# Key-block stores of an attention and key-mix kernel: ACT's DMA queue against SP's

## The chip, the cores and the metric

The kernel runs on one core of a Trainium2 chip. The metric is the device time of one execution in microseconds (us); lower is better. Engines carry the names of the profile: PE (TensorE, matmuls), PEld (its weight loads), DVE (VectorE), ACT (ScalarE), POOL (GpSimd) and SP (SyncE, which here issues DMAs only). SPq and ACTq stand for what an engine's own queue does, such as issuing a DMA.

## What is computed

All data is float32. Attention with a tanh cap runs over 8 batches, 12 heads, 448 positions and 64 columns; its output, with the heads side by side, is the input `x` (448 x 768 per batch) of a gated channel mix.

```python
scores = cap * np.tanh(np.matmul(q, k.transpose(0, 1, 3, 2)) / np.sqrt(64) / cap)
attn = np.exp(scores - np.max(scores, axis=-1, keepdims=True))
x = np.matmul(attn / (np.sum(attn, axis=-1, keepdims=True) + 1e-09), v)
# heads side by side: x is 8 x 448 x 768; x_prev is x one position earlier
xk = mu_k * x + (1.0 - mu_k) * x_prev
xr = mu_r * x + (1.0 - mu_r) * x_prev
k = np.maximum(xk @ w_k, 0.0)
v = k * k @ w_v
out = 1.0 / (1.0 + np.exp(-(xr @ w_r))) * v
```

## The kernel before

**Steps.** The attention part works on 48 pairs of heads (8 batches, six pairs each). `step(i)` (line 818) walks a string of operation names and calls the method of each name, most for pair i and some for an earlier pair: the values' matmuls (V), `gather`, `recip` and `rec_store` for pair i-1, `norm` and the mixes for i-2, `x_store` and `gate_new` for i-3 (lines 824 to 827). Within an engine's queue the order is that of the strings. From step 14 to step 47 the string is made by `rows(i % 6)` out of ROWS and ROWS_PE (lines 64 to 68 and 90 to 92): a prefix such as `25:` keeps a name only where i % 6 is one of these digits, and the PE work of a step stands in two places of the string. Steps 15, 21, 27, 33, 39 and 45 have i % 6 = 3; steps 18, 24, 30, 36 and 42 have 0; steps 14, 20, ... have 2 and 17, 23, ..., 47 have 5.

**A pair's own work.** PE computes transposed scores of four key groups (`scores`, line 261; the first three are L275, the rest of two pairs together L268) into two score buffers, ACT applies tanh (L288) and exp (L301), and PE multiplies with the values (`values`, L312 and L328) into one of two output buffers. DVE's transposing reduction (`red`, L337) sums the exponentials. Four small DMAs on SP gather the sums (`gather`, L343), DVE adds and inverts them (`recip`, lines 347 to 354), SP stores the reciprocals (`rec_store`, L357) and loads them back, spread over all partitions (`rec_load`, L366, two DMAs, at the end of the step). `norm` (L370) of the next step multiplies the output by them. `mix_old` (ACT, L380) and `mix_new` (DVE, L385) form `xk` and free the output buffer of pair i-2, which the values of pair i need. POOL and DVE form the gate's row `xg` (L403, L397), and `x_store` (L414) stores it from SP.

**Key blocks.** The first matrix product of the mix (`xk @ w_k`) runs inside the same steps, one batch late. `krow` (line 473, matmuls L486) multiplies three terms per product in halves of 64 rows and builds key blocks in pairs, in two buffers (`kps`). When a pair of blocks is done, `relu` (ACT, L497) takes it to one of four SBUF tiles `ko` of 128 x 448, and `k_store` (ACT's queue, L503) stores each tile to `k_d` in DRAM, 224 KB. After step 47 the rest of the key matmuls follows, and then the second part (the tail): Strassen-like products of the squared keys and of the gates' rows (L693), with the output stores.

**Weights.** The weights come as 64-bit floats, and steps 0 to 11 and 14 to 41 each turn one piece into float32: `weight_load` (SP, L528), `weight_abs` (ACT, L535), five DVE operations drawn one at a time by the `f` of the string (L559 to L568), a sum on POOL (L575) and `weight_store` (SP, L598) at the end of the step.

**What sets the order around the change.** In steps 15, 18, 21, ... , 45 (i % 6 of 0 and 3) ACT's queue has `relu`, `k_store`, `weight_abs` and then tanh of the next step. In steps 14, 17, ..., 47 (2 and 5) it has `relu` and `k_store` ahead of `mix_old` or tanh 2. SP's queue has, in each step: `load_v`, four `gather`, `weight_load`, `x_store`, `rec_store`, `load_qk`, two `rec_load`, `weight_store`. The steps are counted by their `rec_store`: that of step 24 is issued at 269.87 us of the span, that of step 27 at 304.75 us.

Of the kernel before, what the change touches and what calls it, by code (L numbers as in the profile page):

```python
# [17 lines left out]
B, H, S, D = 8, 12, 448, 64  # L18
# [43 lines left out]
weight_abs load_qk rec_load quad_load tail_open weight_store"""  # L62
EVEN = ODD.replace("V S2", "V S3 S2").replace(" red3", "").replace("tanh2", "tanh3 tanh2").replace("K relu k_store prep\n", "K exp3 red3 relu k_store prep\n")
ROWS = """load_v gather quad_load weight_load PE 135:red3 f f f f f gate_new tanh0 exp0 red0
weight_sum tanh1 exp1 25:relu 25:k_store red1 norm recip x_store rec_store qk_high qk_low 2:mix_old 024:tanh3 tanh2 01345:mix_old mix_new x_high x_low gate_old
exp2 red2 weight_rest weight_sum 024:exp3 024:red3 03:relu 03:k_store weight_abs load_qk rec_load quad_load weight_store PE_END"""
ROWS_PE = (("S1 V S3 S2 K18", "N0 N1 K15"), ("drain V S2 K15", ""), ("S0 S1 W K6 T S3 S2 K18", ""),
           ("S0 S1 V S2 K18", "N0 N1 K12"), ("drain V S3 S2 K18", ""), ("S0 S1 drain V K6 S2 N0 K18", ""))
STEP_0 = """gather rec_load load_v x_store weight_load S0 S1 V0 S2 V1 S3 V2 V3 f f f f f tanh0 exp0 red0
# [39 lines left out]
class Body:  # L109
# [394 lines left out]
        self.ko = []  # L504

    def key_piece(self, n):
        if n < 2 * NARROW:
            return n // 2, range(n % 2 * ND // 2, (n % 2 + 1) * ND // 2)  # L510
        if n >= NWK - 2:
            return (NF - 1, range((n - NWK + 2) * ND // 2, (n - NWK + 3) * ND // 2)) if n < NWK else None
        return n - NARROW, range(ND)
# [544 lines left out]
```

## Time and profile before

| | before |
|---|---|
| median of 3 runs (lowest, highest) | 940.9 us (938.95 to 942.15) |
| the profiled execution, its own time | 941.72 us |
| span of its profile | 939.8 us |
| PE, DVE, ACT, POOL busy, share of the span | 94%, 77%, 66%, 44% |
| ACT's stores of key blocks (L503) | 64 |
| mean granted clock of PE, as a share of full speed | 0.99 |

The span is the time from the first to the last instruction of the profiled execution; the 1.9 us between it and that execution's time lie around it. An engine's share of busy time is a mean over the attention steps (to about 545 us), the rest of the key blocks (to about 580 us) and the tail, which differ. In what follows, "who waited for whom" rows give the total, the number of times and the longest wait; a wait is put down to the event that ended it.

### The profile page before, as it was taken

The page shows a single profiled execution, that of the slowest core. Times are in us where ns is not written, and L with a number is a line of the kernel's source. Part 1 is how long each engine was busy: PE and PEld are TensorE (multiplying, and loading weights), DVE is VectorE, ACT ScalarE, POOL GpSimd, SP SyncE. Part 2 cuts the span into 40 slices and gives each one's busy share as a digit, 9 for nine tenths or more (in the row PEclk, how much of TensorE's full clock was granted, in tenths as well). Part 3 has the DMA queues.
Part 4 walks back from the last instruction along what each step waited for, and adds up shares of the span by engine and source line. Part 5 has one row for each costly group of instructions (what it writes and reads, how often), then busy time and mean ns, then how long its engine had stood idle before and what let it go on. Part 6 is the DMA issues. An engine that isn't in the chain of part 4 may idle for free.

```text
span 939.8 us, 16780 instructions
## 1 busy us (share of the span) xinstructions
PE 883.4 (94%) x5826; PEld 708.8 (75%) x5826; DVE 720.8 (77%) x1246; ACT 622.9 (66%) x907; POOL 409.0 (44%) x345
## 2 busy tenths in 40 slices
PE   7889999899899999999999899999999999999997
PEld 3236667566666666666666589999999999999996
DVE  6888976779779778777868674688878766777775
ACT  8988877667767767776866665655656544555553
POOL 5986565657657667667655200000000013334430
PEclk9999999999999999999999899999999999999999
DMA  5465655575566666657556463754544636767663
GB/s 171 154 214 170 215 157 165 177 211 166 186 205 175 181 192 181 195 174 213 165 156 189 139 227 108 258 158 154 178 146 150 195 120 190 231 204 216 219 214 121
DMA packets 123678, 170.14 MB, mean 181 GB/s; under 512 B 22592, under 2 KB 107712, under 8 KB 123584
## 3 DMA queue, kind: packets, MB, share of 16 engines
q1 hardware_dynamic: 114224, 154.10, 54.0%
q10 hardware_dynamic: 9360, 14.88, 4.3%
q8 instruction: 48, 0.79, 0.4%
q14 instruction: 46, 0.38, 0.1%
HBM read 109.91 MB, written 56.60 MB: 177 GB/s over the span
## 4 chain that ended last, share of the span: by engine, by line
PE 45%; DVE 21%; DMA 17%; ACT 6%; SPq 5%; issue 4%; ACTq 1%; POOL 0%; DVEq 0%
PE ps L693 38%; DVE r L337 7%; DMA r<-rec_d 6%; DMA sq__194<-r 5%; DMA rec_d<-rs 4%; PE kps L462 4%; SPq L343 3%; ACT p L288 3%; ACT p L301 2%; DVE x L370 2%; SPq L366 2%; DVE sq__194 L347 1%; DVE wsq L559 1%; DVE wa L564 1%; DVE wa L562 1%
## 5 line engine op out<-in xcount | busy, mean ns | idle before, releaser
L337 DVE TRANSPOSE_TENSOR_REDUCE r<-p 128x28 f32<-128x896 f32 (+1 forms) x192 | 181.4, 972 | 19.2 <-ACT p L301 18.5
L288 ACT ACTIVATE p<-s,scl_t 128x896 f32<-128x896 f32 (+1 forms) x172 | 166.0, 977 | 27.0 <-PE s L275 7.4
L301 ACT ACTIVATE p<-p,cap_t 128x896 f32<-128x896 f32 (+1 forms) x172 | 174.3, 1023 | 4.3 <-ACT ko L497 0.4
L312 PE MATMUL pv<-p,rv 128*64 128x448 f32 x576 | 126.2, 566 | 21.9 <-DVE xk L385 18.2
L693 PE MATMUL ps<-wvh,hi 128*128 128x384 f32 x392 | 131.0, 334 | 0.0
L693 PE MATMUL ps<-wvl,hi 128*128 128x384 f32 x392 | 130.9, 334 | 0.0
L657 POOL TENSOR_TENSOR s<-src 128x384 f32<-128x384 f32 x14 | 14.2, 1018 | 267.6 <-DVE lo L678 267.6
L486 PE MATMUL kps<-xkh,wkh 64*128 64x448 f32 (+1 forms) x540 | 119.0, 373 | 7.9 <-ACT ko L497 7.9
L677 ACT CAST hi<-s 128x512 fp32r<-128x512 f32 (+1 forms) x112 | 63.6, 568 | 88.7 <-PE ps L693 78.0
L486 PE MATMUL kps<-xkh,wkl 64*128 64x448 f32 (+1 forms) x540 | 116.3, 367 | 0.0
L486 PE MATMUL kps<-xkl,wkh 64*128 64x448 f32 (+1 forms) x540 | 115.1, 364 | 0.0
L678 DVE TENSOR_TENSOR lo<-s,hi 128x512 fp32r<-128x512 f32 (+1 forms) x112 | 70.1, 626 | 57.4 <-ACT hi L677 43.4
L133 POOL TENSOR_TENSOR qkl<-rqk,qkh 128x896 fp32r<-128x896 f32 x47 | 100.2, 2133 | 10.7 <-ACT qkh L127 7.2
L312 PEld LDWEIGHTS pv<-p,rv 128*64 128x64 f32 x576 | 39.4, 140 | 83.4 <-issue 51.3
L575 POOL TENSOR_TENSOR wsq<-wa,wsq 128x384 f32<-128x384 f32 (+1 forms) x40 | 54.2, 1356 | 104.9 <-DVE wsq L568 93.9
L693 PE MATMUL ps<-wrh,hi 128*128 128x384 f32 x294 | 98.6, 335 | 0.3 <-DVE o L716 0.3
L693 PE MATMUL ps<-wrl,hi 128*128 128x384 f32 x294 | 98.5, 335 | 0.0
L677 ACT CAST hi<-src 128x512 fp32r<-128x512 f32 (+1 forms) x84 | 47.7, 567 | 62.1 <-PE ps L693 59.2
L486 PEld LDWEIGHTS kps<-xkh,wkh 64*128 64x128 f32 (+1 forms) x540 | 65.2, 186 | 24.7 <-ACT ko L497 12.7
L693 PE MATMUL ps<-wvh,lo 128*128 128x384 f32 x392 | 83.7, 334 | 0.0
L275 PE MATMUL s<-qkh 64*128 64x448 f32 x288 | 62.0, 418 | 16.0 <-ACT p L288 11.4
L693 PEld LDWEIGHTS ps<-wvh,hi 128*128 128x128 f32 x392 | 73.6, 188 | 0.1
(117 smaller groups left out, 1917.5 us busy)
## 6 DMA issues: line engine op xcount, KB each, us to landing
rqk<-qk SPq DMA_DIRECT2D x47, 448.0 KB
k_d<-ko ACTq DMA_DIRECT2D x64, 224.0 KB
src<-k_d SPq DMA_DIRECT2D x56, 256.0 KB
rv<-v SPq DMA_DIRECT2D x48, 256.0 KB
r<-rec_d SPq DMA_DIRECT2D x96, 112.0 KB
v_d<-o SPq DMA_DIRECT2D x56, 192.0 KB
src<-x_d SPq DMA_DIRECT2D x42, 256.0 KB
vl<-v_d SPq DMA_DIRECT2D x56, 192.0 KB
```

The source lines that it names most:

```text
L133: {"p": self.nc.gpsimd, "v": self.nc.vector}[e].tensor_sub(*a)
L275: nc.tensor.matmul(s[:, (h + i) % 2, 0:S], qk[a][p, k], qk[b][p, 0:S], start=(n == 0), stop=(n == 2))
L288: self.nc.scalar.activation(p32[:, n], self.S.pop((i, g))[:, n, 0:S], AF.Tanh, scale=self.scl_t)
L301: self.nc.scalar.activation(p32, p32, AF.Exp, scale=1.0 if self.maxima else self.cap_t)
L312: nc.tensor.matmul(pv[p, 0:S], v[:, g, h, :], ph[:, (h + i) % 2, :], start=(g == 0), stop=False)
L337: self.nc.vector.tensor_reduce(out=r1[:, 0:RM].rearrange("p (x g) -> p x g", g=3)[:, :, g] if g < 3 else r1[:, RM:RC], in_=p32.rearrange(" ...
L462: nc.tensor.matmul(self.kps[fc][:, 0:S], w, m[:, dc, :], start=first, stop=last)
L486: self.nc.tensor.matmul(self.kps[c][:, 0:S], w[p, dc, c * P:(c + 1) * P], m[p, dc, :], start=s == 0, stop=last or way == 2 and t == 2, ski ...
L575: {"p": self.nc.gpsimd, "v": self.nc.vector}[e].tensor_add(sq, f(a), sq)
L677: self.nc.scalar.copy(hi, x)
L678: self.nc.vector.tensor_sub(lo, x, f(hi))
L693: self.nc.tensor.matmul(o, a[:, c, :], w[:, c, :], start=first and k == 0, stop=last and k == len(todo) - 1, skip_group_check=True)
```

## The change

In steps 14 to 47 the key blocks' stores go out on SP's DMA queue. In steps 14, 17, ..., 47 they follow the `rec_store` of the same step. The blocks that `relu` takes in steps 15, 18, ..., 45 are kept until the next step and are stored there between `x_store` and `rec_store`. `relu` keeps its places. Steps before 14 and after 47 store from ACT's queue as before.

```diff
 ROWS = """load_v gather quad_load weight_load PE 135:red3 f f f f f gate_new tanh0 exp0 red0
-weight_sum tanh1 exp1 25:relu 25:k_store red1 norm recip x_store rec_store qk_high qk_low 2:mix_old 024:tanh3 tanh2 01345:mix_old mix_new x_high x_low gate_old
-exp2 red2 weight_rest weight_sum 024:exp3 024:red3 03:relu 03:k_store weight_abs load_qk rec_load quad_load weight_store PE_END"""
+weight_sum tanh1 exp1 25:relu red1 norm recip x_store 14:k_put rec_store 25:k_put qk_high qk_low 2:mix_old 024:tanh3 tanh2 01345:mix_old mix_new x_high x_low gate_old
+exp2 red2 weight_rest weight_sum 024:exp3 024:red3 03:relu weight_abs load_qk rec_load quad_load weight_store PE_END"""
...
+    def k_put(self):
+        for b, fc, ko in self.ko:
+            self.nc.sync.dma_start(self.k_d[fc, :, b * S:(b + 1) * S], ko)
+        self.ko = []
```

## Rows read from the trace of the kernel before

**Rows 1.** The page, part 1: busy time and share of the whole span.

```profile
PE 883.4 (94%) x5826; PEld 708.8 (75%) x5826; DVE 720.8 (77%) x1246; ACT 622.9 (66%) x907; POOL 409.0 (44%) x345
```

**Rows 2.** Busy time by window: steps 20 to 42, then the tail.

```profile
core 0: us, PE busy (x) PEld busy (x) DVE busy (x) ACT busy (x) POOL busy (x), PEclk, DMA share, GB/s
...
236.00:487.00 251.00, 231.85 (x1870) 163.17 (x1872) 195.63 (x342) 182.16 (x225) 166.06 (x131) 0.99 0.62 186
...
580.00:940.00 360.00, 352.90 (x2035) 352.20 (x2033) 269.88 (x487) 193.07 (x374) 59.96 (x56) 1.00 0.58 182
```

**Rows 3.** The chain of waits, 262 to 330 us: start, us, what.

```profile
269.87 1.89 DMA rec_d<-rs
...
272.31 3.19 DMA r<-rec_d
...
275.58 0.34 ACTq L503
...
276.51 0.50 ACT wsq L535
...
277.09 1.02 ACT p L288
...
304.75 1.55 DMA rec_d<-rs
...
306.86 4.03 DMA r<-rec_d
...
310.96 0.33 ACTq L503
```

**Rows 4.** Timeline of ACT about step 24's end: start, us, line, [idle before].

```profile
269.35 0.95 ACT L497 ACTIVATE ko<-kps 128x448 f32<-128x448 f32 x2
275.58 0.83 ACTq L503 DMA_DIRECT2D k_d<-ko  x2
276.51 0.54 ACT L535 ACTIVATE wsq<-w 128x384 f32<-128x384 f32 x1 [6.21 <-DMA w_d<-wsq]
```

**Rows 5.** Groups by line and shape, 166 to 510 us, with idle before.

```profile
L559 DVE TENSOR_SCALAR wsq<-wsq 128x384 f32<-128x384 f32 x27 | 15.5, 575 | 45.5 <-ACT wsq L535 45.5
...
L535 ACT ACTIVATE wsq<-w 128x384 f32<-128x384 f32 x27 | 14.7, 545 | 49.0 <-DMA r<-rec_d 26.7 <-DMA w_d<-wsq 22.4
```

**Rows 6.** What PE waited for, 150 to 580 us: total, times, longest.

```profile
PE s L275 <- ACT p L288: 9.7, 10, 1.8
PE pv L312 <- DVE xk L385: 9.7, 5, 3.8
PE kps L486 <- ACT ko L497: 7.9, 6, 1.9
PE s L268 <- ACT p L288: 2.3, 4, 0.8
```

**Rows 7.** Busy time by window: granted clock about step 24, and before it.

```profile
264.00:298.00 34.00, 31.98 (x252) 22.66 (x244) 25.61 (x45) 23.22 (x29) 22.50 (x18) 0.95 0.65 185
298.00:332.00 34.00, 30.69 (x252) 22.25 (x250) 27.38 (x51) 25.73 (x33) 22.54 (x18) 1.00 0.64 187
```

**Rows 8.** Timeline of SP, steps 25 and 26.

```profile
280.04 0.33 SPq L414 DMA_DIRECT2D x_d<-xg  x1
284.19 0.36 SPq L357 DMA_DIRECT2D rec_d<-rs  x1
...
293.86 0.33 SPq L357 DMA_DIRECT2D rec_d<-rs  x1
294.32 0.33 SPq L204 DMA_DIRECT2D rqk<-qk  x1
296.26 1.12 SPq L366 DMA_DIRECT2D r<-rec_d  x2
```

**Rows 9.** DMA queues, 166 to 510 us: packets, MB, share of 16 engines.

```profile
q1 hardware_dynamic: 33592, 53.93, 54.2%
q10 hardware_dynamic: 5760, 9.18, 7.3%
```

## The prediction

> **What bounds the kernel now.** I read the busy totals first: TensorE is busy 94% of the span, VectorE 77%, ScalarE 66% [rows 1]. The table by window says where the missing 6% lies: in the tail (580 to 940 us) PE is busy 352.9 of 360 us, but in steps 21 to 42 only 231.85 of 251 us [rows 2]. So the attention steps, where the moved stores are, hold some 19 us of idle PE per 251 us, and no other engine is full there (DVE 195.6, ACT 182.2 of 251).
>
> The chain of waits says what the idle is made of [rows 3]. Around step 24 it hardly touches PE. It runs from the store of the reciprocals (269.87) to their broadcast load, 3.19 us in flight, and from its landing to the **issue of a key block's store on ACT's queue** at 275.58; then weight_abs and the first tanh of the next step run on ACT, DVE follows, and at 304.75 the next such reciprocal store begins the same round. Three steps pass in one round: 34.9 us.
>
> That edge looks odd, since a store of relu's output has nothing to do with the reciprocals. ACT's timeline shows it bare: both relus end at 270.3, the two stores are issued from 275.58 on, and weight_abs has waited 6.21 us [rows 4]. In the program every DMA counts on one of eight completion semaphores and first waits for the last DMA that used the same one; they are dealt out by a timing estimate, by which the stores of steps 15, 18, ... come after that step's rec_load and weight_store. So ACT, whose next work (weight_abs, tanh 0, exp 0) needs none of it, stands still until a DMA has landed that SP issued later. From 166 to 510 us this costs ACT 49.0 us before nine weight_abs, 5.4 us each, and DVE's weight splitting waits 45.5 us behind it [rows 5]. Steps 42 and 45 have the same wait ahead of tanh; eleven in all.
>
> What PE loses is less, since it has matmuls to run meanwhile [rows 6]: 9.7 us in ten waits plus 2.3 in four for a tanh to free a score buffer, and 9.7 in five for mix_new (xk) to free an output buffer. I placed these waits: the fourteen for tanh all come in the step after a stall; four of the five for xk (all but the longest, 3.8 us, at 536 us) come one step later, where DVE is still late. The 7.9 us for relu fall ahead of the stalls of steps 15, 21, ... and are PE's own turn from one pair of key blocks to the next.
>
> **The change, part by part.** *Removed from ACT:* 47 issues (11 stalled pairs; 11 pairs and one triple in steps 14, 17, ... 47). A pair takes 0.83 us of its queue [rows 4]; the stall is the larger part. Terms on PE's path:
> - waits for tanh: 9.7 + 2.3 = 12.0 us go;
> - waits for xk: 9.7 - 3.8 = 5.9 us go, since DVE's weight work starts some 5 us earlier;
> - the clock: after the 1.8 us wait at step 25 the matmuls ran slow; the window 264 to 298 us was granted 0.95, the next one 1.00 [rows 7]. 0.05 x 34 = 1.7 us go.
>
> Together 19.6 us. The unstalled pairs of steps 14, 17, ... sit beside other waits (behind them ACT waits for DVE or for PE's scores, and no PE wait of the list follows them): nothing.
>
> Can the other engines follow? A round without the 5.4 us would need 34.9 - 5.4 = 29.5 us; PE needs 231.85/251 x 34.9 = 32.2 us. So **PE becomes the bound**, with 2.7 us of slack in the round of the reciprocals. ACT's idle falls, but it stays under 80%.
>
> *Added to SP:* 47 issues. A 224 KB row store, the nearest row, takes 0.33 us to issue [rows 8]. In steps 16, 19, ... the pair goes between x_store and rec_store, where SP idles from 280.4 to 284.2 waiting for the reciprocals: 3.8 us hide some 0.8. Queued behind the pair are rec_store and all later SP work; the relu it needs ran a step earlier. In steps 14, 17, ... the pair follows rec_store, and load_qk, rec_load, weight_store, load_v and the next gather stand behind it; SP has 1.6 us before rec_load, which waits for rec_store's landing anyway (load_qk ends at 294.65, rec_load starts at 296.26). Relu ran about 4 us before rec_store there (step 26: it ends by 289.7). So the issues cost 0, and 0.4 us a store if the cover goes.
>
> The completion semaphores turn harmless: with all DMAs of these steps on one queue, the user before is the eighth DMA earlier on SP itself, most of a step back.
>
> *Moved transfers.* ACT's queue moved 40 stores with 7.3% of 344 us of all 16 engines [rows 9], 0.63 us each, 1.26 a pair. On SP's queue they stand in line ahead of the small transfers of the round. From below it costs nothing (the pair has gone while SP idles); from above one pair per three steps lies wholly on the path, 11 x 1.26 = 14 us. A gain is excluded, since the bytes are the same. I take 4 us, nearer to nothing, because the two gaps on SP and the 2.7 us of slack are each larger than 1.26.
>
> The sum: 941.7 (span 939.8 and 1.9 around it) - 19.6 + 4 = 926.1 us. The profiled execution is 0.8 above the median of 940.9, so I forecast **925 us**. Its own range: 941.7 - 19.6 - 0.8 = 921 with no cost, 917 if earlier relus also halve the 7.9 us of PE's turns; 935 with the 14 us.
>
> A rule speaks against this. The Trainium skill, "DMA: Bandwidth & Descriptors", "Issuing engines are not separate DMA queues", holds that starting DMAs on several engines saves only the sequencer's issue time, usually small; the change would then take 47 x 0.4 = 19 us off an ACT that has 27% to spare, and the sum would stay at 941. The trace differs: the queue lost 5.4 us a pair, not 0.8, to a wait. What the rule would give is rival 2.
>
> **Rivals.**
> 1. *The reciprocals' transfers take over part of it.* If queueing takes more than the 2.7 us of slack, waits for tanh go but V waits for xk after every second round: 941 - 12.0 - 1.7 + 4 + about 2 = 933, up to 938. For it: the chain is made of these transfers. Against it: the gaps on SP. 12%.
> 2. *Nothing changes.* ACT's freed time is slack, or the wait travels with the store and SP stands where ACT stood, rec_store behind it: 941. Against it: the chain runs through the stalled issue, and x_store is issued at 280.04, so a wait there would have to be for something issued a step before. 8%.
> 3. *Slower.* Key bytes delay rec_store in one step and rec_load with the next gather in another. With the queues at 54.2 + 7.3 = 62% busy [rows 9], a pair leaves in 1.26/0.38 = 3.3 us; twice per round is 6.6, more than the 5.4 freed. The point is 5.4 us lost per round; at 6.6 it is 11 x 1.2 = 13 us slower, 954. Against it: the pairs start while SP waits on DVE, so part of the 3.3 has passed. 6%. The same page, "Queues, rings and completion order", says that each DMA engine takes a queue's descriptors in ring order and alternates between queues by packet, so small transfers would lose the way past that they have now. No row of before shows it, as these stores never shared SP's queue.
>
> **How the numbers follow.** My forecast has 74%, the rivals 12, 8 and 6. The likeliest is 925 with 917 to 935 of its own; stretched to most of rival 1 the range is 917 to 938 and leaves out some 2 in 10. A measurement of this kernel can tell about 0.3% (2.8 us) from no change. Faster by more: 74 + 12 = 86%; within it 8%; slower 6%.
>
> **What the profile after would show.** Right: no ACT idle of 5 us ahead of weight_abs; DVE's wait for it gone with it; the L275 and L268 waits for tanh mostly gone; PE busy near 97% in the steps; a round near 32.5 us; the tail unchanged. SP's waits ahead of rec_store shorter by the two issues. Wrong: SP waiting 4 us at the new store; r<-rec_d or the gather landing later and x (L370) waiting for it; new PE waits for xk in the steps after 14, 17, .... If ACT's stalls go and PE's idle stays, my step from ACT to PE is what failed.

## The result: 911.05 us, 3.1% faster

| | before | after |
|---|---|---|
| median of 4 runs (lowest, highest) | 939.92 us (938.67 to 942.15) | 911.05 us (909.07 to 913.83) |
| the profiled execution, its own time (span) | 941.72 us (939.8) | 913.83 us (912.0) |
| time after / before, 95% interval | | 0.9692 [0.9658, 0.9727] |

The sign and the mechanism were right; the size was not. I forecast 925 with a range of 917 to 938, and the kernel came out 6 us below the range: a gain of 29 us where I had summed up 16.

The page of the changed kernel, parts 1 and 4 (busy totals, and the chain that ended last by engine):

```profile
PE 880.1 (97%) x5826; PEld 710.1 (78%) x5826; DVE 728.1 (80%) x1246; ACT 623.8 (68%) x907; POOL 409.2 (45%) x345
...
PE 68%; DVE 12%; DMA 9%; ACT 5%; SPq 2%; issue 2%; POOL 0%; DVEq 0%; ACTq 0%; POOLq 0%
```

Against [rows 1], PE rose from 94% to 97% of a shorter span, and PE is now 68% of the chain (45% before). Ten rounds of three steps lie between the rec_store of step 15 and that of step 45; the table by window over just these, for the kernel before and then for the changed one:

```profile
166.69:510.25 343.56, 316.01 (x2550) 221.43 (x2550) 267.99 (x466) 250.81 (x309) 224.50 (x178) 1.00 0.62 185
```

```profile
165.41:484.38 318.97, 313.94 (x2555) 223.46 (x2557) 276.68 (x466) 251.81 (x309) 224.56 (x177) 0.99 0.66 198
```

The columns are those of [rows 2]: window, length, then busy PE, PEld, DVE, ACT, POOL, the clock, DMA share and GB/s. Ten rounds went from 343.6 to 319.0 us, **34.4 to 31.9 us a round**. PE's idle in them fell from 343.56 - 316.01 = 27.6 to 5.0 us, and its busy time by 2.1 us. What is left of the 27.8 us between the spans: 1.3 us was there before step 15 was reached (that point varies between 164.2 and 167.7 us over the runs below, so it is chance), and 1.9 us come later. That last stretch, from the rec_store of step 45 to the end, varies between 425.2 and 430.0 us over the runs, and the run below in which every stall stands has 427.7 there, against 429.6 before and 427.6 after: the 1.9 us are not told from chance either.

ACT's timeline at the end of step 24, as in [rows 4]:

```profile
261.38 0.95 ACT L497 ACTIVATE ko<-kps 128x448 f32<-128x448 f32 x2
262.22 0.56 ACT L540 ACTIVATE wsq<-w 128x384 f32<-128x384 f32 x1
262.67 1.01 ACT L288 ACTIVATE p<-s,scl_t 128x896 f32<-128x896 f32 x1
```

Relu, weight_abs (now L540) and tanh follow each other without a gap, where 6.21 us stood. The groups by line from 165 to 484 us say the same of all steps, as [rows 5] did for before:

```profile
L564 DVE TENSOR_SCALAR wsq<-wsq 128x384 f32<-128x384 f32 x27 | 19.9, 736 | 0.1
L540 ACT ACTIVATE wsq<-w 128x384 f32<-128x384 f32 x27 | 14.8, 548 | 0.0
```

Of the 49.0 us of ACT and the 45.5 us of DVE nothing is left. What PE waits for from 160 to 515 us, as in [rows 6]:

```profile
PE kps L486 <- ACT ko L497: 3.2, 3, 1.6
PE pv L312 <- DVE xk L385: 3.1, 2, 2.8
```

The waits for tanh (9.7 + 2.3 us) are gone altogether, those for xk are down to one long one in the last steps, and those for relu fell from 7.9 to 3.2, which I had not expected. SP in steps 25 and 26, as in [rows 8], the new stores being L510:

```profile
270.87 0.83 SPq L510 DMA_DIRECT2D k_d<-ko  x2
273.16 0.37 SPq L357 DMA_DIRECT2D rec_d<-rs  x1
273.62 0.35 SPq L204 DMA_DIRECT2D rqk<-qk  x1
...
283.03 0.34 SPq L357 DMA_DIRECT2D rec_d<-rs  x1
283.46 0.80 SPq L510 DMA_DIRECT2D k_d<-ko  x2
284.35 0.41 SPq L204 DMA_DIRECT2D rqk<-qk  x1
284.86 1.12 SPq L366 DMA_DIRECT2D r<-rec_d  x2
```

A pair takes 0.8 us of SP. In step 25 SP still waits from 271.7 to 273.2 for the reciprocals; in step 26 rec_load now starts right behind load_qk. The old gap there is used up, but not overdrawn.

### The profile page after: what moved, and what is told of

It reads as the page before. It is cut to its first block, busy times and chain, and to the rows that moved or that the text cites. A ratio compares the mean times of both kernels' runs of the same rounds, so it can differ in the third digit from the quotient of the medians.

```text
span 912.0 us, 16778 instructions
## 1 busy us (share of the span) xinstructions
PE 880.1 (97%) x5826; PEld 710.1 (78%) x5826; DVE 728.1 (80%) x1246; ACT 623.8 (68%) x907; POOL 409.2 (45%) x345
## 4 chain that ended last, share of the span: by engine, by line
PE 68%; DVE 12%; DMA 9%; ACT 5%; SPq 2%; issue 2%; POOL 0%; DVEq 0%; ACTq 0%; POOLq 0%
PE ps L698 39%; PE kps L486 10%; PE pv L312 7%; DVE r L337 5%; PE s L275 4%; PE kps L462 4%; DMA r<-rec_d 3%; DMA sq__194<-r 3%; ACT p L288 2%; SPq L343 2%; ACT p L301 2%; DMA rqk<-qk 2%; PE pv L328 1%; DMA rec_d<-rs 1%; PE s L268 1%
## 5 line engine op out<-in xcount | busy, mean ns | idle before, releaser
L683 DVE TENSOR_TENSOR lo<-src,hi 128x512 fp32r<-128x512 f32 (+1 forms) x84 | 56.7, 675 | 21.4 <-ACT hi L682 19.3
```

Source lines behind the costliest of these rows:

```text
L683: self.nc.vector.tensor_sub(lo, x, f(hi))
```

## Experiments

My theory: the whole gain is that ACT no longer waits for a DMA that is issued later, and the queue on which the stores go is of no matter. The rivals: the gain is ACT's issue time; or the stores had to leave ACT's queue; and, for the size, that the moved bytes cost something. Each run is named by what it does; the first four ran beside the kernel before at 938.27 us.

**Only the stalled pairs, or only the others.** The operations of ROWS that differ from the changed kernel, first run and second:

```diff
-25:relu red1 norm recip x_store 14:k_put rec_store 25:k_put qk_high
+25:relu 25:k_store red1 norm recip x_store 14:k_put rec_store qk_high
```

> Only the pairs of steps 15, 18, ..., 45 go out on SP (one step later); those of steps 14, 17, ..., 47 are issued on ACT as before. Wait theory (all the gain is ACT no longer standing 5 us until rec_load or weight_store has landed): 23 of 47 stores moved bring nearly all of it, 909 to 915 us, and ACT's wait ahead of weight_abs is gone. Issue theory (the gain is ACT's time for issuing 47 stores): about half, 922 to 929.

Measured 912.27 us, ratio 0.9731 [0.9705, 0.9758].

```diff
-x_store 14:k_put rec_store 25:k_put qk_high
+x_store rec_store 25:k_put qk_high
...
-03:relu weight_abs
+03:relu 03:k_store weight_abs
```

> Only the stores of steps 14, 17, ..., 47 go out on SP, behind rec_store; the pairs of steps 15, 18, ... stay on ACT. Wait theory: the stalls stay, ACT idles some 5 us ahead of nine weight_abs, 935 to 942 us. Issue theory: about half of the gain, 922 to 929.

Measured 937.69 us, ratio 1.0001 [0.9981, 1.002]. ACT's waits from 160 to 515 us in it (total, times, longest):

```profile
ACT wsq L540 <- DMA r<-rec_d: 26.5, 5, 5.7
ACT wsq L540 <- DMA w_d<-wsq: 20.9, 4, 5.9
ACT p L288 <- DMA rv<-v: 6.3, 1, 6.3
ACT p L288 <- DMA r<-rec_d: 4.6, 1, 4.6
```

All eleven stalls stand there, 58.3 us, and 25 stores taken off ACT's queue bought nothing. The 22 stores of the other kind (the 23 of the expectation is a miscount; the last triple is left on ACT) bring it all: within the intervals the first run is as fast as the changed kernel. The issue theory falls.

**The same without SP.** From the kernel before:

```diff
-weight_sum tanh1 exp1 25:relu 25:k_store
+weight_sum tanh1 exp1 14:k_store 25:relu 25:k_store
...
-03:relu 03:k_store weight_abs
+03:relu weight_abs
```

> All stores stay on ACT's queue; the pairs of steps 15, 18, ... are issued one step later, behind exp 1, where the DMAs whose completion they wait for were issued most of a step before. Wait theory: it is the wait and not the queue, so most of the gain comes without SP, 911 to 920 us, the rest being 0.8 us of issue a pair. Theory that the stores must leave ACT's queue (issue time, or two queues in each other's way): no gain, 935 to 942.

Measured 910.45 us, ratio 0.9706 [0.9679, 0.9732]. ACT's timeline at the same place:

```profile
261.07 0.98 ACT L497 ACTIVATE ko<-kps 128x448 f32<-128x448 f32 x2
261.94 0.56 ACT L535 ACTIVATE wsq<-w 128x384 f32<-128x384 f32 x1
...
266.11 1.93 ACTq L503 DMA_DIRECT2D k_d<-ko  x2
268.92 1.01 ACT L288 ACTIVATE p<-s,scl_t 128x896 f32<-128x896 f32 x1 [2.48 <-PE s L275]
```

The pair is issued on ACT's own queue at 266.1, where ACT would wait for PE's scores anyway. So no store had to change its queue: what counts is that it is issued where the DMA it has to wait for is already done. SP is one such place.

**The wait put back without a store.** The changed kernel, with a small copy on ACT that waits for rec_load (the old stalls ended with the landing of rec_load or of weight_store, which is issued behind it):

```diff
+    def peek(self):
+        t = self.up.tile([P, 8], F32, name="peek", bufs=1)
+        self.nc.scalar.copy(t, max(self.R.items())[1][:, 0:8])
...
-03:relu weight_abs load_qk rec_load quad_load
+03:relu 1245:weight_abs load_qk rec_load 03:peek 03:weight_abs quad_load
```

> The changed kernel with all stores on SP, and in steps 15, 18, ..., 45 ACT copies eight columns of the freshly loaded reciprocals just ahead of weight_abs, so that it waits for rec_load as before but issues no store. Wait theory: the loss comes back, ACT idle near 5 us a step with it, PE waits for tanh near 12 us, for xk near 6 and for relu near 7, 934 to 942 us. If the gain came from the stores' queue or their issue: 911 to 916.

Measured 926.21 us, ratio 0.9874 [0.985, 0.9899]: between the two, so neither expectation held. The waits of ACT and then those of PE, 160 to 515 us:

```profile
ACT peek L510 <- DMA r<-rec_d: 48.0, 11, 5.4
```

```profile
PE kps L486 <- ACT ko L497: 6.5, 5, 1.3
PE pv L312 <- DVE xk L385: 6.3, 5, 1.4
PE s L275 <- ACT p L288: 4.9, 7, 1.2
```

The wait that I put back is smaller than the old one: 48.0 us in eleven, with the copy 4.6 us each, where the old stalls took 58.5 us, 5.3 each, store issue included. The loss came back in the same three places, the waits for relu among them (6.5 us, where the changed kernel has 3.2); those go with the stall. But 86% of the stall brought back only 15 of 29 us. That pointed to two limits: a round lasts the longer of what PE needs and of what the round of the reciprocals needs with the stall in it, and the first part of a stall is free.

**A stall of a chosen length.** The changed kernel with four, then eight dummy copies on ACT in the place of the old wait:

```diff
+    def filler(self):
+        if not self.scr:
+            self.scr.append(self.up.tile([P, S], F32, name="scr", bufs=1))
+            self.nc.gpsimd.memset(self.scr[0], 0.0)
+        for _ in range(4):
+            self.nc.scalar.copy(self.scr[0], self.scr[0])
...
-03:relu weight_abs
+03:relu 03:filler weight_abs
```

> The changed kernel with four dummy copies on ACT (128 x 448, some 0.55 us each, 2.2 us together) ahead of weight_abs in steps 15, 18, ..., 45, in the place of the old wait. Two-limits theory: a round lasts the longer of PE's 31.9 us (measured after the change) and 29.0 us (the 34.4 of before less its 5.3 of stall) plus what ACT loses there; 2.2 us stay under the slack of 2.9, so 910 to 916. Theory that every us lost there costs its 11 us: 934.

> The same with eight copies, some 4.4 us: 29.0 + 4.4 = 33.4, 1.5 over PE's 31.9, eleven times: 16 us, 924 to 932. Theory that every us costs: 958. Theory that PE hides it: 911 to 915.

Measured 914.48 us (0.9745 [0.9715, 0.9776]) and 933.23 us (0.9944 [0.9924, 0.9965]), beside 938.34 of before. One copy took 0.57 us. The first 2.3 us a round cost some 3.5 us in all (its interval just overlaps that of the changed kernel), the next 2.3 us cost 18.8. Eight were 1 us above my band. The mean of ten rounds (rec_store of step 15 to that of step 45), against "29.0 plus the loss, or PE's 31.9, whichever is longer", where 29.0 is 34.4 less 5.3:

| kernel | ACT loses a round | the rule gives | measured |
|---|---|---|---|
| before | 5.3 us | (set) | 34.4 us |
| the wait put back | 4.6 | 33.6 | 33.3 |
| eight copies | 4.5 | 33.5 | 34.0 |
| four copies | 2.3 | 31.9 | 32.1 |
| changed | 0 | (set) | 31.9 |
| stores later on ACT | 0 | 31.9 | 31.5 |

The rule holds within 0.5 us. Part of that is scatter: a second profile of the changed kernel, of the last set of runs below, gave 31.6 us a round.

**The price of the moved bytes.** Every moved block stored twice, the second time to a scratch tensor:

```diff
             self.nc.sync.dma_start(self.k_d[fc, :, b * S:(b + 1) * S], ko)
+            self.nc.sync.dma_start(self.k_e[fc, :, b * S:(b + 1) * S], ko)
```

> The changed kernel, each key block of steps 14 to 47 stored twice on SP (the second time to a scratch tensor): twice the issues and bytes ahead of rec_store, rec_load and the gather. Theory that the moved transfers cost nothing, because the round of the reciprocals has slack: 910 to 915 us. Theory that the 4 us of the forecast are real and hidden behind other gains: one more pair costs at least 4, up to 14 us, 915 to 926.

Measured 928.65 us, ratio 0.9901 [0.9871, 0.9932], 17.6 us more than the changed kernel (which was measured in another set of runs; by the two ratios it is 19.6) and above both bands. DVE's waits in it and then PE's, 160 to 515 us:

```profile
DVE sq__195 L347 <- DMA sq__195<-r: 27.2, 19, 2.4
DVE x L370 <- DMA r<-rec_d: 5.5, 8, 1.6
```

```profile
PE kps L486 <- ACT ko L497: 12.2, 7, 3.2
PE pv L312 <- DVE xk L385: 1.6, 4, 0.6
```

In the changed kernel the first of these was 19.8 us (5.9 before the change) and the second absent:

```profile
DVE sq__194 L347 <- DMA sq__194<-r: 19.8, 20, 2.0
```

So the small transfers of the round do come later with twice the stores, DVE's norm (L370) waits for them, and PE waits 12.2 us for relu. SP in step 26 of this run, to be read against the changed kernel's rows above:

```profile
290.78 0.34 SPq L357 DMA_DIRECT2D rec_d<-rs  x1
...
293.09 1.49 SPq L204 DMA_DIRECT2D rqk<-qk  x1
294.67 1.12 SPq L366 DMA_DIRECT2D r<-rec_d  x2
```

From rec_store to rec_load SP needs 3.89 us here, and 1.83 in the changed kernel: the four stores take their issue time, and load_qk's issue behind them takes 1.49 us in place of 0.41. So the run doubles issues and bytes at once, and does not tell which of the two makes the round late.

What one pair's bytes do can be read from the traces by timing rec_load from its issue to its landing (the last count on its completion semaphore), in the mean of steps 17, 20, ..., 44. It took 3.30 us before the change, 4.57 in the changed kernel, where a pair stands in line ahead of it, and 4.29 with the doubled stores; where no pair stands between rec_store and rec_load (the places exchanged, stores later on ACT), 3.4 to 3.6. So a pair in line delays rec_load by some 1.3 us, close to the 1.26 of the prediction's upper bound, and at the single dose the round's slack hides it.

**The place on SP**, with the two places exchanged:

```diff
-x_store 14:k_put rec_store 25:k_put
+x_store 25:k_put rec_store 14:k_put
```

> The changed kernel with the order on SP turned round: the stores of steps 14, 17, ... ahead of rec_store, those of 16, 19, ... behind it. Theory that the place on SP does not matter within the slack: 909 to 914 us. Theory that it was chosen on an edge: 915 or more, with SP waiting ahead of rec_store or rec_load longer.

Measured 908.74 us, ratio 0.9676 [0.9646, 0.9706]. It looked 2 us better, so it ran again beside three others, all on one chip, with the kernel before at 940.33 us. The fourth has the stores ahead of step 14 and behind step 47 on SP too (`k_store` with `nc.sync` for `nc.scalar`).

> The changed kernel once more, on the chip of the next three: 907 to 914 us. It is the yardstick for them.

> The turned order on SP (stores of steps 14, 17, ... ahead of rec_store, of 16, 19, ... behind it) once more. Theory that the place on SP does not matter: within 0.3% of the changed kernel. Theory that the place takes the last of PE's idle: 2 to 3 us faster, as it looked.

> All stores on ACT's queue, the stalled pairs a step later, once more. Theory that the queue does not matter, only the wait: within 0.3% of the changed kernel.

> The changed kernel with the stores ahead of step 14 and behind step 47 on SP too. No stall of ACT stands there in the trace of after, so within 0.3% of the changed kernel; slower if SP, full of the tail's loads after step 47, stands at a store that waits for relu.

| kernel | median | ratio to before, 95% interval |
|---|---|---|
| changed | 910.71 us | 0.9684 [0.966, 0.9708] |
| places exchanged | 910.96 | 0.9692 [0.9669, 0.9716] |
| stores later on ACT | 913.52 | 0.971 [0.9683, 0.9738] |
| all stores on SP | 913.1 | 0.972 [0.969, 0.975] |

The exchange is worth nothing; the first difference was scatter. The other two are some 2.5 us, 0.3%, behind with intervals that overlap the changed kernel's: not told apart. None of them beats the changed kernel. In the trace of the later stores on ACT, ACT stood once 5.7 us at a pair (step 45's, at 491 us; the profile names no releaser) and once 2.5 us until a key block's store had landed, so that place is not free of stalls in every step.

## Why the prediction was wrong, point by point

**The mechanism held; the sum failed.** The eleven stalls, what releases them, the DVE work behind them, the eight completion semaphores turning harmless, and PE as the next bound: each was seen, and the runs with half the stores and with a later issue on ACT show that the stall alone makes the gain. Of the semaphores the traces show this: DMAs land on eight of them in both kernels; the stalled store at 275.58 us uses that of the rec_load which SP had issued at 272.31; in the changed kernel the user before was issued on SP 4.6 to 7.4 us earlier, and SP issues none of the 47 stores more than 0.13 us after the issue ahead of it.

Rival 2 (nothing changes) is refuted. Its rule, the Trainium skill's "DMA: Bandwidth & Descriptors", "Issuing engines are not separate DMA queues", says that another issuing engine saves only issue time. The run with only the unstalled stores moved agrees with that, 25 issues off ACT for nothing (937.69 us against 938.27); the rule does not count what an issue may have to wait for, and here that was the whole gain. Rival 1 did not come about, since the waits for xk fell. Nor did rival 3: even twice the stores left the kernel no slower than before.

**The terms that held:** the waits for tanh, 12.0 us forecast and 12.0 gone; those for xk, 5.9 forecast and 5.6 gone (3.1 left, 2.8 of it the late one). The issues on SP cost nothing that shows: the runs without SP are no faster.

**The terms that failed:**
- "The 7.9 us for relu ... are PE's own turn": most of them were not. They fell to 3.2 us, and came back with the stall (6.5), with eight copies (7.1) and with the doubled stores (12.2). That is 4.7 us. The first of the six, in step 15, lies ahead of all eleven stalls and stayed (1.9 us before, 1.6 after). How the stall reaches the others is open. Ahead of relu ACT has mix_old, which waits for DVE's norm, but that wait alone does not explain it. In step 27 it is the same in both kernels, and so is PE's wait behind it; here is ACT's mix_old and then PE, before the change and after it:

```profile
303.39 0.64 ACT L380 ACTIVATE pv<-x,om_k 128x448 f32<-128x448 f32 x1 [1.34 <-DVE x L370]
305.47 0.90 PE L486 MATMUL kps<-xkh,wkh 64*128 64x448 f32 x2 [1.24 <-ACT ko L497]
```

```profile
292.34 0.64 ACT L380 ACTIVATE pv<-x,om_k 128x448 f32<-128x448 f32 x1 [1.33 <-DVE x L370]
294.43 0.90 PE L486 MATMUL kps<-xkh,wkh 64*128 64x448 f32 x2 [1.24 <-ACT ko L497]
```

  The waits of steps 21, 39 and 45 are gone, and that of step 33 fell from 1.4 to 0.3 us.
- The clock, 1.7 us: none of it went. The slow stretch only moved, from behind the 1.8 us wait for tanh at 278 us to behind the 1.6 us wait for relu at 165 us. In each profile it was granted 0.50 (1.2 of 2.4 GHz), from 279 to 282 us before and from 167 to 169 us after. The row of the changed kernel, columns as in [rows 2], to be read against the 0.95 of [rows 7]:

```profile
165.41:197.00 31.59, 31.16 (x242) 21.73 (x244) 27.49 (x44) 24.02 (x30) 22.74 (x18) 0.95 0.64 186
```

  The run with only the unstalled stores moved was granted 1.00 over its ten rounds with every stall in place, so the slow stretch does not come with the stalls. PE's busy time fell by 2.1 us all the same, and no row says why.
- "I take 4 us" for the moved transfers: a pair in line does delay rec_load by 1.3 us, but off the path, and the time shows nothing of it.
- The choice of the sum itself. 19.6 - 4 = 15.6 us came from a list of PE's waits, of which I let some stand. But the same text had both limits of a round, 34.9 us now and 32.2 us of PE work, and said that PE becomes the bound. Their difference, 2.7 us, times eleven rounds is 29.7 us, and 941.7 - 29.7 - 0.8 = 911.2. The measured rounds are near it: 34.4 - 31.9 = 2.5 us, 24.6 for ten, and the eleventh. The two workings contradicted each other by 14 us, and I took the one that I could itemise.

That 911.2 comes so close to 911.05 is luck in part: the 34.9 us is one round, longer than the mean; 5.0 us of PE's idle stayed in the ten rounds where this working leaves none; and 3.2 us of the difference between the profiles lie outside the rounds. The list itself, with the waits as they went, gives 12.0 + 5.6 + 4.7 = 22.3 us and 941.7 - 22.3 - 0.8 = 918.6. Of the remaining 7.5 us, PE's shorter busy time is 2.1 and what lies outside the rounds is 3.2. Another 2.0 come from the profiled execution of the changed kernel, which was 2.8 us above its median where I took off 0.8.

The range went wrong with these terms: its lower end let the relus give back half and no more.

## What to carry to other kernels

Where a chain of waits closes on itself round after round, and the next limit is known, the gain is about (round now - next limit) x rounds; a sum over the bound engine's visible waits is only a check, and a contradiction between the two has to be resolved before a number is given. A wait of the bound engine that comes earlier in the step than the stall may still go with the stall: let none stand in the sum without a reason that a row shows. And where a DMA is issued decides what its queue stands still for: look at what releases the instruction behind the issue, and if it is an unrelated DMA, move the issue to where that DMA has long landed, on any queue.

## What the runs showed that I had not expected

- The response to the stall has a knee: 2.3 us of ACT's time a round cost some 3.5 us over eleven rounds, 4.5 us cost some 22.
- The changed kernel's DMA schedule is near its own knee: 47 more stores of 224 KB, issues and bytes together, cost 17.6 us although the queues' share rose only from 66% to 70% of a window, and the first 47 cost nothing that shows. The windows of the run with doubled stores and ten rounds, columns as above:

```profile
166.67:501.06 334.39, 318.87 (x2558) 225.82 (x2560) 278.81 (x466) 252.39 (x310) 224.87 (x177) 0.98 0.70 217
```

  PE's clock was granted 0.98 there against 0.99, and its busy time rose by 4.9 us for the same matmuls; longer waits for relu go before it, but no run separates the two.
